# A fused attention and MLP kernel: the softmax epsilon added on ScalarE, and the split of the sinks' values spread over two iterations

## The chip, the cores and the metric

The kernel runs on one core of a Trainium2 chip. The metric is device time in microseconds (us), lower is better. TensorE (PE) multiplies matrices, VectorE (DVE), ScalarE (ACT) and GpSimd (POOL) work elementwise, SyncE (SP) issues DMAs. Each engine takes its instructions strictly in its own order; semaphores hold an instruction until what it needs is there.

## The reference, cut to what matters

A sliding-window attention with sink columns (2 batches, 8 heads, 768 positions, head size 64; 4 sinks, window 128) feeds a gated MLP with a spatial mixing, and that a second mixer. Only the attention's softmax is touched:

```
scores = np.where(keep, scale * q @ k.T, -1e9)
scores = scores - np.max(scores, axis=-1, keepdims=True)
a = np.exp(scores)
a = a / (np.sum(a, axis=-1, keepdims=True) + 1e-09)
out = a @ v                      # then x @ w_in, layer norm, w_spatial, w_out, two more MLPs
```

## The kernel before, in words

The method `banded` does the attention. A block `j` is 128 queries of one batch (12 blocks); a group `g` is half of a block's heads (four heads, 24 groups). A loop over `n` from -3 to 25 is a software pipeline: iteration `n` transposes the probabilities of group `n` on TensorE (`a_transpose`, tile `tr`) and evicts them (`a_out`: `aT` by ScalarE, `aL` by VectorE), normalises group `n+1` (`sums`, `norm`), computes the scores of group `n+3` (`qk` on TensorE into `sc`, `scores` on VectorE into `s` with the negated row minimum `nm`), takes the exponentials of group `n+2` (`expo` on ScalarE, which also accumulates the four row sums into `sums`), and multiplies group `n-1` with the values (`pv`). Every second iteration a finished block is split into a high and a low part (`x_out`: `xTH`, `xTL`), and the sink columns are prepared (`sink_parts`, `sinks`: `eS`, `fl`, `aS`) and multiplied with the sinks' values `vs` (`sinks_mm`, L320).

Two things lie between. `pump` converts one slab of float64 weights per iteration for n = -1 to 6 (three VectorE instructions, L481, L485, L488, into `wi`; then `flush` in the next iteration: ScalarE `wvH` or `wuH`, L499, and GpSimd `wvL` or `wuL`, L500). `fill` gives TensorE tiles of the first MLP (`psv`, `psu`) as soon as the blocks they need are ready, with a fixed budget per iteration; their evictions are `vf` and `uT` on ScalarE, with the layer norm (`st`, `vf`, `vnH`, `vnL`) on VectorE, ScalarE and GpSimd. The order on each engine is the order of the code: the scheduler is set to manual.

The row sums become reciprocals in `sums`, two small VectorE instructions (L195 and L196, 24 of each). `norm` waits for the reciprocals: GpSimd scales heads 2 and 3 of the group (L246), ScalarE heads 0 and 1 (L250). After that ScalarE goes on to the next exponentials (L234, each followed by a read of its accumulator).

`split_vs` is called twice, in iterations 1 and 13, once per batch: ScalarE copies the sinks' values rounded into `vs` (L156), and VectorE subtracts that from the raw values for 32 of the partitions (L158). The raw values stand in one of the four buffers of the tag `tmp`, which `wi` uses too.

Of the kernel before, what the change touches and what calls it, by code (L numbers as in the profile page):

```python
# [8 lines left out]
F32R = mybir.dt.float32r  # L9
I32 = mybir.dt.int32  # L10
U32 = mybir.dt.uint32
AF = mybir.ActivationFunctionType
ALU = mybir.AluOpType
PSUM = bass.MemoryType.PSUM

P = 128
B, H, S, D = 2, 8, 768, 64
NB = S // P
DM = H * D
# [5 lines left out]
SK = 8  # L25
SR = 3 * 4 * SK
# [10 lines left out]
def f32(ap):  # L37
    return ap.bitcast(F32)


class Kernel:
# [106 lines left out]
            nc.sync.dma_start(out=raw[0:SR], in_=self.vs[b])  # L148
            self.vsraw = raw

    def split_vs(self, b):

        nc = self.nc
        raw = self.vsraw
        t = self.vsb[b] = self.ap.tile([P, DM], F32R, name="vs", tag="vs", bufs=1)
        nc.scalar.activation(out=t[0:SR], in_=raw[0:SR], func=AF.Copy)  # L156
        r = slice(4 * SK, 8 * SK)
        nc.vector.tensor_tensor(out=t[r], in0=raw[r], in1=f32(t[r]), op=ALU.subtract)  # L158

    def slots(self, j):  # L160

# [28 lines left out]
    def sums(self, g):  # L190

        V = self.nc.vector
        r = self.ap.tile([P, 4], F32, name="r", tag="r", bufs=3)
        self.rs[g] = r
        V.tensor_scalar(out=r, in0=self.sm[g], scalar1=1e-9, scalar2=None, op0=ALU.add)  # L195
        V.reciprocal(r, r)  # L196

    def scores(self, g):

# [23 lines left out]
    def expo(self, g):  # L223
        nc = self.nc
        j, ph = divmod(g, 2)
        i = j % NB
        u = KW if i else P
        s, nm = self.ss[g]
        if ph == 0:
            self.e[j] = self.ap.tile([P, H, KW], F32, name="e", tag="e", bufs=2)  # L230
        sm = self.ap.tile([P, 4], F32, name="sums", tag="sums", bufs=3)
        self.sm[g] = sm
        for c in range(4):
            nc.scalar.activation(  # L234
                out=self.e[j][:, 4 * ph + c, :u], in_=s[:, c, :u], func=AF.Exp, bias=nm[:, c : c + 1], scale=-1.0,
                accum_out=sm[:, c : c + 1],
            )

    def norm(self, g):

        nc = self.nc
        j, ph = divmod(g, 2)
        r = self.rs[g]
        w = KW if j % NB else P
        e = self.e[j][:, 4 * ph : 4 * ph + 4, 0:w]
        nc.gpsimd.tensor_tensor(  # L246
            out=e[:, 2:4], in0=e[:, 2:4], in1=r[:, 2:4].unsqueeze(2).to_broadcast([P, 2, w]), op=ALU.mult
        )
        for c in range(2):
            nc.scalar.activation(out=e[:, c], in_=e[:, c], func=AF.Copy, scale=r[:, c : c + 1])  # L250
# [88 lines left out]
    def banded(self):  # L339
        self.q, self.vb, self.vsb, self.ps_s, self.ss, self.e, self.sm, self.rs = {}, {}, {}, {}, {}, {}, {}, {}  # L340
        self.aT, self.ps_x, self.aS, self.dv, self.eS = {}, {}, {}, {}, {}
        NJ = B * NB
        self.kr = self.ap.tile([P, NC4, RING, KW], F32, name="kr")
        self.vf = self.ap, "vf", 2
        self.scalar_loads(self.cp)
        self.load_qk(0, 2)
        self.warm(10)
        self.load_qk(1)
        self.prefetch()
        self.load_v(0)  # L350
        self.load_qk(2)
        self.masks(self.ap)
        for n in range(-LQ, NG + 2):
            j, ph = divmod(n, 2)
            self.xdone = self.xnext
            if ph and n >= -1:
                if (n + 7) // 2 < NJ:
                    self.load_qk((n + 7) // 2)
                if (n + 3) // 2 < NJ:
                    self.load_v((n + 3) // 2)  # L360
            if 0 <= n + LN < NG:
                self.sums(n + LN)
            if 0 <= n < NG:
                self.a_transpose(n)
                self.a_out(n)
            if 0 <= n + LN < NG:
                self.norm(n + LN)
            if n + LQ < NG:
                self.qk(n + LQ)
                if n < 0:  # L370
                    self.warm(3)
                self.scores(n + LQ)
            if 0 <= n + LE < NG:
                self.expo(n + LE)
            if 0 <= n < NG and ph == 0 and j % NB:
                self.v_step(j)
                self.sink_parts(j)
            if n in (1, 13):
                self.split_vs(n // 12)
            self.step()  # L380
            if n in PUMPS:
                self.pump()
            if n == max(PUMPS) + 1:
                self.flush()
            if 0 <= n - 1 < NG:
                self.pv(n - 1)
                if ph == 0:
                    if (j - 1) % NB:
                        self.sinks_mm(j - 1)

                    self.fill_until(j - 1)
                    self.x_out(j - 1)
            if 0 <= n < NG and ph == 1 and j % NB:
                self.sinks(j)
            if n == NG - 4:
                self.raws = [self.spatial_load(r) for r in range(2)]
            self.fill(BUDGET)
        self.xdone = self.xnext
        self.vf = self.sp, "tmp", 4
# [529 lines left out]
```

## Time and profile before

| | |
|---|---|
| median of 3 runs | 494.08 us (492.68 to 495.11) |
| the profiled execution's own time | 494.1 us |
| its span, first to last instruction | 492.3 us |
| busy: PE, DVE, ACT, POOL | 469.2, 281.2, 178.8, 146.7 us |
| granted TensorE clock, mean over the span | 0.979 |

The attention occupies about the first 140 us; the rest of the span is the MLPs, where TensorE is busy almost throughout. The shares of the whole span say little about the first stage, so it is read on its own below. A row of a timeline gives start, duration, engine, line, operation, and in square brackets how long the engine was idle before it and whom it waited for.

### The profile page before, as it was taken

How to read it: one execution, taken by the hardware profiler on the slowest of the kernel's cores; microseconds unless marked ns; L12 is line 12 of the kernel's file. 1: busy time of each engine (PE TensorE's matmuls, PEld its weight loads, DVE VectorE, ACT ScalarE, POOL GpSimd, SP SyncE). 2: the span in 40 equal slices, each digit the busy share in tenths (PEclk: the TensorE clock that was granted, in tenths of full speed). 3: DMA queues.
4: the chain of work that ended last, by engine and by line, in shares of the span. 5: the costliest groups of instructions: out<-in, count | busy, mean ns of one | idle time of the engine just before them, and what ended most of it. 6: DMA issues, size and time to landing. Idle time of an engine off the chain costs nothing.

```text
span 492.3 us, 6952 instructions
## 1 busy us (share of the span) xinstructions
PE 469.2 (95%) x2562; PEld 392.3 (80%) x2562; DVE 281.2 (57%) x633; ACT 178.8 (36%) x483; POOL 146.7 (30%) x164
## 2 busy tenths in 40 slices
PE   8678899999999999999999989999999999999994
PEld 7356588788898999998888768888888888888883
DVE  5899865775555399937878698666412211311112
ACT  4656777787754323225642122222101210010000
POOL 1355752354354556642543033222100000000000
PEclk9859899999999999999999999999999999999998
DMA  8744132202005023303534044222010000200002
GB/s 258 246 151 152 66 101 95 87 22 87 1 30 185 1 85 87 102 6 116 173 119 137 35 129 128 91 94 73 21 66 1 0 1 0 86 1 0 1 0 92
DMA packets 19722, 38.48 MB, mean 78 GB/s; under 512 B 1824, under 2 KB 8224, under 8 KB 19680
## 3 DMA queue, kind: packets, MB, share of 16 engines
q1 hardware_dynamic: 19248, 37.69, 23.5%
q8 instruction: 22, 0.36, 0.3%
q10 hardware_dynamic: 432, 0.26, 0.2%
q14 instruction: 20, 0.16, 0.1%
HBM read 34.80 MB, written 3.15 MB: 77 GB/s over the span
## 4 chain that ended last, share of the span: by engine, by line
PE 81%; DVE 11%; ACT 5%; issue 1%; POOL 1%; POOLq 0%; ACTq 0%
PE pso L60 7%; PE pso L58 7%; PE pso L59 7%; PE psc L58 6%; PE psc L60 6%; PE psc L59 6%; PE psg L60 3%; PE psg L59 3%; PE psg L58 3%; PE pv L301 3%; PE ps L60 2%; PE ps L58 2%; PE ps L59 2%; ACT e L234 2%; DVE wi L485 2%; PE psu L58 2%
## 5 line engine op out<-in xcount | busy, mean ns | idle before, releaser
L647 DVE SCALAR_TENSOR_TENSOR hh<-psc,hh 128x512 fp32r<-128x512 f32 x36 | 24.9, 691 | 124.6 <-ACT hh L646 124.6
L646 ACT ACTIVATE hh<-psc 128x512 fp32r<-128x512 f32 x36 | 21.5, 597 | 156.0 <-PE psc L60 156.0
L60 PE MATMUL pso<-c2H,hh 128*128 128x512 f32 x144 | 56.3, 391 | 1.9 <-DVE hh L647 1.9
L58 PE MATMUL pso<-c2H,hh 128*128 128x512 f32 x144 | 56.8, 394 | 0.0
L59 PE MATMUL pso<-c2L,hh 128*128 128x512 f32 x144 | 56.1, 390 | 0.0
L488 DVE SCALAR_TENSOR_TENSOR wi<-rawi,wi 128x512 int32<-128x512 int32 (+2 forms) x46 | 40.3, 876 | 1.6
L234 ACT ACTIVATE e<-s,nm 128x136 f32<-128x136 f32 (+1 forms) x96 | 37.6, 393 | 3.9 <-DVE nm L218 3.9
L485 DVE SCALAR_TENSOR_TENSOR wi<-rawi,wi 128x512 int32<-128x512 int32 (+2 forms) x46 | 36.4, 791 | 1.6
L481 DVE TENSOR_SCALAR wi<-rawi 128x512 int32<-128x512 int32 (+2 forms) x46 | 33.4, 726 | 0.7 <-DMA rawi<-in_moe_w_ch 0.5
L60 PEld LDWEIGHTS pso<-c2H,hh 128*128 128x128 f32 x144 | 27.0, 188 | 8.0 <-DVE hh L647 2.3
L58 PE MATMUL psg<-wsTH,vnH 128*128 128x384 f32 x96 | 32.1, 334 | 0.0
L59 PE MATMUL psg<-wsTL,vnH 128*128 128x384 f32 x96 | 32.1, 334 | 0.0
L60 PE MATMUL psg<-wsTH,vnL 128*128 128x384 f32 x96 | 32.1, 334 | 0.0
L500 POOL TENSOR_TENSOR c2L<-wi,c2H 128x512 fp32r<-128x512 f32 x12 | 16.1, 1339 | 52.4 <-ACT c2H L499 52.4
L59 PEld LDWEIGHTS pso<-c2L,hh 128*128 128x128 f32 x144 | 27.1, 188 | 5.4
L58 PEld LDWEIGHTS pso<-c2H,hh 128*128 128x128 f32 x144 | 27.0, 188 | 5.3
L188 PE MATMUL sc<-kr,q 64*128 64x264 f32 (+2 forms) x192 | 28.8, 419 | 0.4 <-DVE nm L218 0.2
L60 PE MATMUL psc<-u2H,c 128*128 128x512 f32 x72 | 28.0, 389 | 0.0
L58 PE MATMUL psc<-u2H,c1H 128*128 128x512 f32 x72 | 28.0, 389 | 0.0
L59 PE MATMUL psc<-u2L,c1H 128*128 128x512 f32 x72 | 28.0, 389 | 0.0
L60 PE MATMUL psc<-u2H,c1L 128*128 128x512 f32 x72 | 28.0, 389 | 0.0
L58 PE MATMUL psc<-u2H,c 128*128 128x512 f32 x72 | 28.0, 389 | 0.0
(143 smaller groups left out, 1120.1 us busy)
## 6 DMA issues: line engine op xcount, KB each, us to landing
rawi<-in_moe_w_ch SPq DMA_DIRECT2D x24, 512.0 KB, 3.4
rawi<-in_moe_w_in SPq DMA_DIRECT2D x8, 512.0 KB, 4.5
v<-in_v SPq DMA_DIRECT2D x12, 256.0 KB, 3.6
out_x<-o SPq DMA_DIRECT2D x12, 256.0 KB, 2.4
kr<-in_k SPq DMA_DIRECT2D x11, 272.0 KB, 4.1
q<-in_q SPq DMA_DIRECT2D x11, 256.0 KB, 4.2
raws<-in_w_spT SPq DMA_DIRECT2D x6, 384.0 KB, 4.5
rawi<-in_moe_w_out SPq DMA_DIRECT2D x4, 512.0 KB, 5.2
```

The source lines that it names most:

```text
L58: self.nc.tensor.matmul(ps, lh, rh, start=(first and i == 0), stop=False)
L59: self.nc.tensor.matmul(ps, lh, rl, start=False, stop=False)
L60: self.nc.tensor.matmul(ps, ll, rh, start=False, stop=(last and i == n - 1))
L188: nc.tensor.matmul(o, q[r, p, :], k, start=True, stop=True)
L234: nc.scalar.activation(out=self.e[j][:, 4 * ph + c, :u], in_=s[:, c, :u], func=AF.Exp, bias=nm[:, c : c + 1], scale=-1.0, accum_out=sm[:, ...
L301: nc.tensor.matmul(ps[h * D : (h + 1) * D, p, :], w[:, (2 * p + h) * D : (2 * p + h + 1) * D], self.aT[g][c][:, 2 * x + h, :], start=(p == ...
L481: V.tensor_scalar(out=wi, in0=hi, scalar1=3, scalar2=0x3FFFFFFF, op0=ALU.logical_shift_left, op1=ALU.bitwise_and,)
L485: V.scalar_tensor_tensor(out=wi, in0=hi, scalar=-0x40000000, in1=wi, op0=ALU.bitwise_and, op1=ALU.bitwise_or)
L488: V.scalar_tensor_tensor(out=wi, in0=lo, scalar=29, in1=wi, op0=ALU.logical_shift_right, op1=ALU.bitwise_or)
L500: self.nc.gpsimd.tensor_tensor(out=dl, in0=w, in1=f32(dh), op=ALU.subtract)
L646: nc.scalar.activation(out=h, in_=ps, func=AF.Relu)
L647: nc.vector.scalar_tensor_tensor(out=l, in0=ps, scalar=0.0, in1=f32(h), op0=ALU.max, op1=ALU.subtract)
```

## The change

The addition of 1e-9 leaves VectorE: `expo` ends with one ScalarE instruction that adds it to the four row sums in place (24 times), and `sums` is a reciprocal alone. `split_vs` is called in two parts: the copy on ScalarE in iterations 2 and 14, the subtraction on VectorE in iterations 3 and 15.

```
 def split_vs(self, b, part):
     raw = self.vsraw
+    if part == 0:
         t = self.vsb[b] = self.ap.tile([P, DM], F32R, name="vs", tag="vs", bufs=1)
         nc.scalar.activation(out=t[0:SR], in_=raw[0:SR], func=AF.Copy)
+    else:
+        t = self.vsb[b]
         r = slice(4 * SK, 8 * SK)
         nc.vector.tensor_tensor(out=t[r], in0=raw[r], in1=f32(t[r]), op=ALU.subtract)
...
 def sums(self, g):
-    V.tensor_scalar(out=r, in0=self.sm[g], scalar1=1e-9, scalar2=None, op0=ALU.add)
-    V.reciprocal(r, r)
+    V.reciprocal(r, self.sm[g])
...
 def expo(self, g):
     for c in range(4):
         nc.scalar.activation(... func=AF.Exp, ..., accum_out=sm[:, c : c + 1])
+    nc.scalar.activation(out=sm, in_=sm, func=AF.Copy, bias=1e-9)
...
-            if n in (1, 13):
-                self.split_vs(n // 12)
+            if n in (2, 3, 14, 15):
+                self.split_vs(n // 12, n % 2)
```

How the instructions now stand, at three places. In the changed kernel line numbers are two or three higher (L196 is L198, L218 is L220, L250 is L253, L481 is L484). First VectorE in iteration 1, from the last score to the reciprocals of group 2 and on; before:

```order
L218 ISA s,nm<-sc,m_141 128x136
L218 ISA nm 128x1
L158 TENSOR_TENSOR vs<-vsraw,vs 32x512 [waits DMAHW0_49,Activation_49]
L481 TENSOR_SCALAR wi<-rawi 128x512 [waits DMAHW1_49]
L485 SCALAR_TENSOR_TENSOR wi<-rawi,wi 128x512 [waits DVE_49]
L488 SCALAR_TENSOR_TENSOR wi<-rawi,wi 128x512 [waits DVE_49]
L195 TENSOR_SCALAR r<-sums 128x4 [waits Pool_49]
L196 RECIPROCAL r<-r 128x4 [waits DVE_49]
L278 TENSOR_TENSOR aL<-tr,lowT 128x512 [waits Activation_49]
```

The same place on VectorE in the changed kernel:

```order
L220 ISA s,nm<-sc,m_141 128x136
L220 ISA nm 128x1
L484 TENSOR_SCALAR wi<-rawi 128x512 [waits DMAHW1_49]
L488 SCALAR_TENSOR_TENSOR wi<-rawi,wi 128x512 [waits DVE_49]
L491 SCALAR_TENSOR_TENSOR wi<-rawi,wi 128x512 [waits DVE_49]
L198 RECIPROCAL r<-sums 128x4 [waits Activation_49,Pool_49]
L281 TENSOR_TENSOR aL<-tr,lowT 128x512 [waits Activation_49]
```

The subtraction with its wait for ScalarE is gone from here, and one of the two small instructions in front of `aL`. Next ScalarE, from the exponentials of iteration 1 to those of iteration 2 and what follows; before:

```order
L234 ACTIVATE e,sums<-s,nm 128x136 x4
L156 ACTIVATE vs<-vsraw 96x512 [waits DMAHW0_49]
L499 ACTIVATE wvH<-wi 128x512
L275 ACTIVATE aT<-tr 128x512 [waits PE_49]
L250 ACTIVATE e<-e,r 128x136 [waits DVE_49,Activation_49]
L250 ACTIVATE e<-e,r 128x136 [waits Activation_49]
L234 ACTIVATE e,sums<-s,nm 128x136 [waits Pool_49]
L234 ACTIVATE e,sums<-s,nm 128x136 x3
L257 ACTIVATE eS<-e 128x2x32 [waits Activation_49,Pool_49]
L499 ACTIVATE wvH<-wi 128x512
L329 ACTIVATE xTH<-pv 128x4x128 [waits PE_49]
```

The same place on ScalarE in the changed kernel:

```order
L236 ACTIVATE e,sums<-s,nm 128x136 x4
L240 ACTIVATE sums<-sums 128x4 [waits Activation_49]
L502 ACTIVATE wvH<-wi 128x512
L278 ACTIVATE aT<-tr 128x512 [waits PE_49]
L253 ACTIVATE e<-e,r 128x136 [waits DVE_49]
L253 ACTIVATE e<-e,r 128x136
L236 ACTIVATE e,sums<-s,nm 128x136 [waits Pool_49]
L236 ACTIVATE e,sums<-s,nm 128x136 x3
L240 ACTIVATE sums<-sums 128x4 [waits Activation_49]
L260 ACTIVATE eS<-e 128x2x32 [waits Pool_49]
L157 ACTIVATE vs<-vsraw 96x512 [waits DMAHW0_49]
L502 ACTIVATE wvH<-wi 128x512
```

A new instruction (L240) that waits for ScalarE's own accumulators stands behind each group's exponentials, and the copy `vs` now stands in front of the `wvH` and `xTH` of iteration 2. Last VectorE in iteration 3, before:

```order
L218 ISA s,nm<-sc,m_141 128x136
L218 ISA nm 128x1
L481 TENSOR_SCALAR wi<-rawi 128x512 [waits DMAHW6_49]
L485 SCALAR_TENSOR_TENSOR wi<-rawi,wi 128x512 [waits DVE_49]
L488 SCALAR_TENSOR_TENSOR wi<-rawi,wi 128x512 [waits DVE_49]
L195 TENSOR_SCALAR r<-sums 128x4 [waits Activation_49,Pool_49]
L196 RECIPROCAL r<-r 128x4 [waits DVE_49]
```

And the same place on VectorE in the changed kernel:

```order
L220 ISA s,nm<-sc,m_141 128x136
L220 ISA nm 128x1
L161 TENSOR_TENSOR vs<-vsraw,vs 32x512 [waits DMAHW0_49]
L484 TENSOR_SCALAR wi<-rawi 128x512 [waits DMAHW6_49,Pool_49]
L488 SCALAR_TENSOR_TENSOR wi<-rawi,wi 128x512 [waits DVE_49]
L491 SCALAR_TENSOR_TENSOR wi<-rawi,wi 128x512 [waits DVE_49]
L198 RECIPROCAL r<-sums 128x4 [waits Activation_49]
```

The subtraction stands here now, ahead of the weight conversion, and the first conversion waits for GpSimd as well, since its buffer is another one of the four.

## Rows read from the trace of the kernel before

**Rows 1.** Stretches: length, busy PE, PEld, DVE, ACT, POOL; granted clock, DMA share, GB/s

```profile
10.00:21.20 11.20, 7.19 (x54) 4.50 (x52) 10.28 (x41) 7.64 (x30) 3.62 (x4) 1.00 1.02 335
21.20:34.90 13.70, 9.46 (x50) 6.28 (x47) 12.16 (x38) 9.05 (x33) 6.64 (x8) 0.50 0.43 145
34.90:55.30 20.40, 16.58 (x130) 11.83 (x130) 19.62 (x56) 13.38 (x46) 12.78 (x15) 1.00 0.40 131
55.30:58.80 3.50, 3.50 (x22) 2.87 (x23) 3.40 (x11) 1.63 (x8) 3.00 (x5) 0.51 0.01 2
57.00:165.00 108.00, 106.98 (x782) 89.51 (x781) 65.70 (x230) 73.54 (x235) 50.12 (x73) 0.99 0.21 69
```

**Rows 2.** PE's waits from 12 to 160 us: total, times, longest

```profile
PE pv L301 <- DVE xTL L330: 4.4, 4, 1.6
PE tr L267 <- ACT e L250: 4.0, 2, 2.3
PE tr L267 <- DVE aL L278: 3.5, 2, 3.3
PE psu L58 <- ACT aS L313: 0.6, 1, 0.6
```

**Rows 3.** PE in order of time, three of its waits

```profile
55.18 0.57 PE L301 MATMUL pv<-aT,v 128*64 128x128 f32 x4 [1.58 <-DVE xTL L330]
...
69.29 0.44 PE L58 MATMUL psu<-xTH,wuH 128*128 128x384 f32 x1 [0.57 <-ACT aS L313]
...
107.93 0.44 PE L301 MATMUL pv<-aT,v 128*64 128x128 f32 x4 [0.18 <-DVE xTL L330]
```

**Rows 4.** Busy time of line 195 alone, 12 to 57 us

```profile
12.00:57.00 45.00, 3.70 (x8) 0.83 0.52 170
```

**Rows 5.** VectorE in order of time, 14 to 31 us

```profile
14.15 0.16 DVE L195 TENSOR_SCALAR r<-sums 128x4 f32<-128x4 f32 x1
14.35 0.18 DVE L196 RECIPROCAL r<-r 128x4 f32<-128x4 f32 x1
...
18.02 1.23 DVE L195 TENSOR_SCALAR r<-sums 128x4 f32<-128x4 f32 x1
...
22.39 0.68 DVE L158 TENSOR_TENSOR vs<-vsraw,vs 32x512 fp32r<-32x512 f32 x1 [1.13 <-ACT vs L156]
23.10 1.43 DVE L481 TENSOR_SCALAR wi<-rawi 128x512 int32<-128x512 int32 x1
...
30.97 0.64 DVE L195 TENSOR_SCALAR r<-sums 128x4 f32<-128x4 f32 x1
```

**Rows 6.** GpSimd in order of time, 17 to 61 us

```profile
17.48 1.75 POOL L500 TENSOR_TENSOR wvL<-wi,wvH 128x512 fp32r<-128x512 f32 x1 [2.19 <-ACT wvH L499]
...
22.95 1.29 POOL L500 TENSOR_TENSOR wvL<-wi,wvH 128x512 fp32r<-128x512 f32 x1 [2.77 <-ACT wvH L499]
...
53.94 1.72 POOL L551 TENSOR_TENSOR vnL<-vf,vnH 128x512 fp32r<-128x512 f32 x1
...
60.10 1.27 POOL L500 TENSOR_TENSOR wuL<-wi,wuH 128x512 fp32r<-128x512 f32 x1 [1.64 <-ACT wuH L499]
```

**Rows 7.** VectorE in order of time, 55 to 60 us

```profile
55.05 0.68 DVE L542 BATCH_NORM_STATS2 st<-vf 128x6 f32<-128x512 f32 x1
...
60.08 0.18 DVE L196 RECIPROCAL r<-r 128x4 f32<-128x4 f32 x1
```

**Rows 8.** ScalarE in order of time, around 28 and 90 us

```profile
28.45 0.19 ACT L234 ACTIVATION_READ_ACCUMULATOR e<-s,nm 128x1 f32 x1
28.55 0.24 ACT L257 ACTIVATE eS<-e 128x64 fp32r<-128x64 f32 x1
...
90.25 0.62 ACT L156 ACTIVATE vs<-vsraw 96x512 fp32r<-96x512 f32 x1
90.77 0.58 ACT L532 ACTIVATE vf<-psv 128x512 f32<-128x512 f32 x1
```

**Rows 9.** DMA issues of the weights: count, size, median us to landing

```profile
rawi<-in_moe_w_in SPq DMA_DIRECT2D x8, 512.0 KB, 4.5
```

More of the change, by code (lines that the diff above doesn't have):

```diff
@@ L149, in load_v @@
             self.vsraw = raw
-    def split_vs(self, b):
+    def split_vs(self, b, part):
         nc = self.nc
         raw = self.vsraw
[L155 to L158, printed above, removed]
+        if part == 0:
+            t = self.vsb[b] = self.ap.tile([P, DM], F32R, name="vs", tag="vs", bufs=1)
+            nc.scalar.activation(out=t[0:SR], in_=raw[0:SR], func=AF.Copy)
+        else:
+            t = self.vsb[b]
+            r = slice(4 * SK, 8 * SK)
+            nc.vector.tensor_tensor(out=t[r], in0=raw[r], in1=f32(t[r]), op=ALU.subtract)
     def slots(self, j):
@@ L194, in sums @@
         self.rs[g] = r
-        V.tensor_scalar(out=r, in0=self.sm[g], scalar1=1e-9, scalar2=None, op0=ALU.add)
-        V.reciprocal(r, r)
+        V.reciprocal(r, self.sm[g])
     def scores(self, g):
@@ L237, in expo @@
             )
+        nc.scalar.activation(out=sm, in_=sm, func=AF.Copy, bias=1e-9)
     def norm(self, g):
@@ L377, in banded @@
                 self.sink_parts(j)
-            if n in (1, 13):
-                self.split_vs(n // 12)
+            if n in (2, 3, 14, 15):
+                self.split_vs(n // 12, n % 2)
             self.step()
```

## The prediction

> **What bounds the kernel now.** I read the busy times by stretch first, since shares of the whole span mix stages [rows 1]. From 57 to 165 us TensorE is busy 106.98 of 108 us: whatever VectorE saves there is hidden, and the MLPs behind it are TensorE's too. From 21.2 to 55.3 us it is the other way round: VectorE is busy 12.16 of 13.7 and 19.62 of 20.4 us, and TensorE leaves 4.2 and 3.8 us empty. TensorE's waits say for whom [rows 2]: for `xTL` and `aL`, which are VectorE's, and for ScalarE's scaled probabilities, which wait for VectorE's reciprocals. They come to 11.9 us, of which the last one inside the attention's first third ends at 55.18 us [rows 3]. So the change is worth what it takes off VectorE's chain before 55 us, less what it puts on ScalarE where TensorE waits for ScalarE afterwards: 0.57 us at 69.29 for `aS`, and 0.18 us at 107.93 for `xTL` [rows 3].
>
> **The additions that leave VectorE.** From 12 to 57 us there are 8 of them, busy 3.70 us [rows 4]; the last stands behind the wait that ends at 55.18 us and counts for nothing, so 7. An undisturbed one costs VectorE 0.20 us, from its start at 14.15 to the reciprocal's start at 14.35 [rows 5]: 7 x 0.20 = 1.4 us. Two of the seven were held: the one at 18.02 took 1.23 instead of 0.16 us and ended at 19.25, when GpSimd's `wvL` ended (17.48 + 1.75 = 19.23) [rows 5, 6]; the one at 30.97 took 0.64. That is another 1.07 + 0.48 = 1.55 us, but only if the reciprocal that now stands in that place is not held the same way. No row shows a reciprocal that starts under a GpSimd operation with two inputs, so this is bounded: 0 to 1.55 us. Two rows speak for 1.55. The statistics at 55.05, one input from SBUF, ran 0.55 us under `vnL` (until 55.66) and took 0.68 us as ever [rows 6, 7]. And the `wuL` that began at 60.10, 20 ns into the reciprocal of 60.08, took 1.27 us, no more than the free one at 22.95 (1.29), so the reciprocal held nothing against GpSimd either [rows 6, 7]. I take 1.55.
>
> The Trainium skill, "SBUF — State Buffer", section "Who interferes with whom", says that VectorE and GpSimd exclude each other on one shared pair of ports, that copies, casts and tensor_scalar can enter the two-port modes that need it, and that an instruction outside these modes with at most one SBUF input does not contend. The trace agrees for the held additions (1.23 us under `wvL`) and for the statistics (0.68 us under `vnL`). The page does not name the reciprocal among either; by this rule it is free if it has no two-port mode, and held if it has one, which is the second case below.
>
> **The wait that leaves iteration 1.** VectorE sat idle 1.13 us for ScalarE's `vs` ahead of 22.39 [rows 5]: all of that goes, since in iteration 3 the copy is an iteration old. The subtraction itself (0.68 us) is only moved, from one VectorE-bound iteration to another: 0. The conversion behind it took 1.43 us from 23.10, held by the `wvL` of 22.95 to 24.24 [rows 5, 6]: 1.1 us at most. Without wait and subtraction VectorE gets to the conversions some 1.8 us sooner, and the `wvL`, which had to wait for `wvH` behind `vs` on ScalarE, comes only some 0.3 us sooner; it then falls under the third conversion as in iteration 0, and GpSimd waits instead. 0 to 1.1, I take 1.0.
>
> **What ScalarE gets.** The new instruction has four elements; the nearest rows are the accumulator read of one (0.19 us) and `eS` of 64 (0.24 us) [rows 8]. It must wait for the last accumulator: `eS` started 0.10 us after that read began, while the new one can start only when it has ended, 0.19 us plus a hand-over of about 0.035 us (the gap between addition and reciprocal, 14.31 to 14.35). What follows it on ScalarE is then 0.19 + 0.035 + 0.10 - 0.10 = about 0.23 us later; the upper bound, with nothing overlapped, is 0.19 + 0.035 + 0.24 = 0.47. The reciprocal could wait for it: 0 to 0.23 us each. I take 0 in the first stage, since no addition there shows a wait [rows 5] and ScalarE is busy 9.05 of 13.7 us [rows 1]. Queued behind it are `wvH`/`wuH`, `xTH`, `aS`, `vf`. In iteration 2 the copy `vs` (0.52 us from 90.25 to the next start [rows 8]) is ahead of `xTH` too: 0.75 us in all, of which `xTL` loses between 0 and 0.75, as far as `xTH` had no lead; ScalarE's idle third of that stretch makes me take 0.2. In iteration 3 GpSimd's half of a weight comes 0.23 later and the conversions, one subtraction later, fall under it: 0 to 1.1 (the hold of 23.10); I take 0.2, as if they had been held before too.
>
> First stage: 1.4 + 1.55 + 1.13 + 1.0 - 0.4 = 4.7 us off VectorE's chain.
>
> **What TensorE can take of it.** From 21.2 to 34.9 us its granted clock is 0.50, the 1.2 GHz level, after a stretch in which it was busy 7.19 of 11.2 us [rows 1]. That earlier stretch hardly changes, so I expect the same low level. If VectorE runs 4 us ahead by 31 us, up to 4 us of TensorE's work that was done at the full level moves into the low one and takes twice as long for half of the room: 0 to 2 us lost, I take 1.1. So 3.6 us by 55 us. The next to be late would be the weights, 4.5 us from issue to landing [rows 9]; with two buffers they are asked for nearly two iterations ahead, and an undisturbed one takes 3.67 us (14.35 to 18.02 [rows 5]), so two take 7.3: I take 0.
>
> **Given back after 57 us.** TensorE's wait at 69.29 is for `aS`, directly behind exponentials: + 0.23; the like place one block later, for which the list has no wait, 0 to 0.23: + 0.23. Toward 107.93 a chain of ScalarE and VectorE runs through iterations 13 to 17; it loses the second wait for `vs`, gets the copy (0.52) in iteration 14, the subtraction in 15 and 0.23 three times, and saves 0.20 per reciprocal: + 0.5. Bounds for all this: 0 (if TensorE has work in hand) to 3.7, below. Sum 1.0.
>
> Total: -3.6 + 1.0 = -2.6. The profiled execution took 494.1 us, 1.8 more than its span and within 0.1 of the median 494.08: 494.1 - 2.6 = 491.5 us.
>
> **Rivals.**
> Second case, the reciprocal is held like the addition. Then 1.55 falls away, and in iteration 1 a new hold of about 1.3 us appears behind a `wvL` that now runs past the conversions: 4.7 - 1.55 - 1.3 = 1.85, less 0.5 for the low clock, less 1.0 later: -0.4, 493.7 us. For it: nothing measured under GpSimd; against it: `wuL` at 60.10.
>
> Third, ScalarE becomes the bound after 57 us. If each of the 14 iterations from 8 to 21 passes its 0.23 us on to TensorE, and the chain to 107.93 its 0.5: 3.2 + 0.5 = 3.7, so +0.1, 494.2 us. For it: the wait for `aS`, where there is no lead. Against it: ScalarE is busy 73.54 of 108 us there [rows 1]. The Trainium skill speaks against the change here: "ScalarE: Activation LUTs", section "Rules for kernel authors", puts adds on VectorE, not ScalarE; the section "What ACT_TABLE_LOAD costs" gives 186 ns plus 0.833 ns per element with immediate operands, an estimate of 0.19 us here, which no run so far shows.
>
> Fourth, more than forecast: the second low stretch, 55.3 to 58.8 us at 0.51 with TensorE busy throughout [rows 1], goes away because TensorE idles less before it. That gives 1.7 us more: 489.8 us.
>
> Fifth, slower: the shifted pattern costs TensorE another stretch at 1.2 GHz like that of 13.7 us, where it has work throughout; half of it is 6.85 us: 491.5 + 6.85 = 498.3. It decides if TensorE, at some place ahead of it, idles as it does from 10 to 21 us (busy 0.64); nothing in the change adds such idle time, which speaks against it.
>
> **How the numbers follow.** Forecast 0.45 (its own range 490.3 to 493.0), second 0.12, third 0.15, fourth 0.20, fifth 0.08. About 0.5%, 2.5 us, is what a measurement can tell from no change, so the border lies at 491.6, next to the forecast, which I split 0.25 faster and 0.20 same. Faster: 0.25 + 0.20 = 0.45; same: 0.20 + 0.12 + 0.15 = 0.47; slower 0.08. The range runs from 489.4, under the fourth case's middle, to 495.0, over the third's; the fifth and the tail of the fourth are left out.
>
> **What would show it.** Reciprocals of 0.18 us under `wvL`; no wait of VectorE for `vs`; TensorE's waits before 57 us down from about 12 to about 8 us; the new instruction near 0.19 us with what follows 0.23 us later; waits for `aS` of about 0.8 and 0.3 us. I am wrong if a reciprocal takes over 0.5 us, if VectorE waits for ScalarE's sums before 55 us, or if the granted clock after 57 us has a new low stretch.

## The result: 488.8 us, twice the forecast gain

The changed kernel takes 488.77 us (median of 4 runs, 487.84 to 489.52) against 494.08 us: a ratio of 0.989, 95% interval 0.9865 to 0.9914, or 4.2 to 6.7 us less. The forecast was 2.6 us less. The profiled execution took 489.52 us, the longest of the four, at a span of 487.7 us, 4.6 us less than that of before; its trace shows where they are.

The stretches of [rows 1] in the changed kernel, and below them three stretches at one granted clock each (columns as there):

```profile
10.00:21.20 11.20, 8.21 (x58) 4.70 (x56) 10.61 (x42) 9.43 (x37) 3.43 (x5) 0.96 1.03 342
21.20:34.90 13.70, 12.73 (x80) 9.01 (x80) 12.95 (x41) 10.35 (x39) 9.92 (x10) 0.66 0.50 166
34.90:55.30 20.40, 17.59 (x124) 12.76 (x125) 17.93 (x59) 14.87 (x53) 14.61 (x18) 0.92 0.36 113
...
57.00:165.00 108.00, 106.16 (x774) 89.85 (x771) 60.84 (x200) 72.08 (x234) 47.58 (x68) 1.00 0.22 69
...
20.40:30.60 10.20, 9.23 (x48) 5.89 (x45) 9.86 (x33) 8.67 (x31) 7.74 (x8) 0.50 0.63 211
30.70:51.10 20.40, 17.59 (x146) 12.84 (x145) 19.43 (x57) 14.58 (x51) 13.63 (x16) 1.00 0.41 131
51.20:54.50 3.30, 3.30 (x9) 2.50 (x8) 2.14 (x12) 2.54 (x11) 2.59 (x5) 0.50 0.01 2
```

From 10 to 35 us TensorE did 138 matmuls instead of 104: the same work came sooner. The first stretch at 1.2 GHz is there again, but ends at about 30.6 instead of 34.9 us. The second is there too, 4 us sooner; so the fourth rival did not come about, though its figure, 489.8 us, lies nearer to the measured time than the forecast's. VectorE is still the full engine from 30.7 to 51.1 us, 19.43 of 20.4. Behind 57 us TensorE is empty for 1.84 us where before it was for 1.02.

TensorE's waits from 12 to 160 us (total, times, longest), to be held against [rows 2], and four of them in order of time, against [rows 3]:

```profile
PE pv L304 <- DVE xTL L333: 3.7, 4, 1.7
PE tr L270 <- ACT e L253: 2.4, 2, 1.5
PE psu L58 <- ACT aS L316: 1.1, 2, 0.8
...
```

```profile
49.62 0.44 PE L304 MATMUL pv<-aT,v 128*64 128x128 f32 x4 [1.75 <-DVE xTL L333]
...
63.97 0.44 PE L58 MATMUL psu<-xTH,wuH 128*128 128x384 f32 x1 [0.81 <-ACT aS L316]
...
74.38 0.44 PE L58 MATMUL psu<-xTH,wuH 128*128 128x384 f32 x1 [0.32 <-ACT aS L316]
...
103.20 0.44 PE L304 MATMUL pv<-aT,v 128*64 128x128 f32 x4 [0.54 <-DVE xTL L333]
```

The `pv` that began at 55.18 us begins at 49.62: 5.56 us sooner. 0.35 us of that lie ahead of iteration 0's first transpose (11.28 after 11.63 us) and are put down to the execution, not to the change: the other kernels start it at 11.14 to 11.50 us, those that keep every addition on VectorE (split_only, before_late) at 11.19 and 11.17. 5.2 us are the change's. The wait in front of this `pv` is still for `xTL`, and no shorter (1.75 after 1.58): TensorE does not limit here. Its waits before 57 us fell from 11.7 to 6.2 us, where about 8 were forecast. Then some is given back: `aS` at 63.97 is waited for 0.24 us longer than at 69.29 before, the one at 74.38 is new, and the wait at 103.20 is 0.36 us longer. From there to the end the lead is 4.7 us.

VectorE from 13 to 26 us, its reciprocals and the first conversion of iteration 2, and GpSimd's weights and `dv` beside them, against [rows 5, 6]:

```profile
13.79 0.17 DVE L198 RECIPROCAL r<-sums 128x4 f32<-128x4 f32 x1
...
17.46 0.17 DVE L198 RECIPROCAL r<-sums 128x4 f32<-128x4 f32 x1
...
21.13 0.17 DVE L198 RECIPROCAL r<-sums 128x4 f32<-128x4 f32 x1
...
23.63 0.85 DVE L484 TENSOR_SCALAR wi<-rawi 128x512 int32<-128x512 int32 x1
...
26.45 0.16 DVE L198 RECIPROCAL r<-sums 128x4 f32<-128x4 f32 x1
```

```profile
17.09 1.59 POOL L503 TENSOR_TENSOR wvL<-wi,wvH 128x512 fp32r<-128x512 f32 x1 [2.44 <-ACT wvH L502]
...
20.78 1.58 POOL L503 TENSOR_TENSOR wvL<-wi,wvH 128x512 fp32r<-128x512 f32 x1 [1.50 <-ACT wvH L502]
...
22.92 1.27 POOL L288 TENSOR_TENSOR dv<-v 128x512 f32<-128x512 f32 x1
```

The reciprocals at 17.46 and 21.13 start inside a `wvL` (17.09 to 18.68, 20.78 to 22.36) and take 0.17 us. From reciprocal to reciprocal, iterations 0 and 1 take 3.67 us each, where they took 4.94 and 6.80 in the kernel before (from 14.35 to 19.29, and from there to 26.09):

```profile
19.29 0.18 DVE L196 RECIPROCAL r<-r 128x4 f32<-128x4 f32 x1
...
26.09 0.18 DVE L196 RECIPROCAL r<-r 128x4 f32<-128x4 f32 x1
```

Iteration 2 has a new hold: its first conversion starts under the `dv` of 22.92 and takes 0.85 instead of 0.42 us.

### The profile page after: what moved, and what is told of

It reads as the page before. It is cut to its first block, busy times and chain, and to the rows that moved or that the text cites. A ratio compares the mean times of both kernels' runs of the same rounds, so it can differ in the third digit from the quotient of the medians.

```text
span 487.7 us, 6920 instructions
## 1 busy us (share of the span) xinstructions
PE 469.0 (96%) x2562; PEld 391.9 (80%) x2562; DVE 274.5 (56%) x609; ACT 183.2 (38%) x507; POOL 147.0 (30%) x164
## 4 chain that ended last, share of the span: by engine, by line
PE 82%; DVE 9%; ACT 5%; issue 1%; POOL 1%; POOLq 0%; ACTq 0%
PE pso L60 7%; PE pso L58 7%; PE pso L59 7%; PE psc L60 6%; PE psc L59 6%; PE psc L58 6%; PE psg L60 3%; PE psg L59 3%; PE psg L58 3%; PE pv L304 3%; PE ps L60 2%; PE ps L58 2%; PE ps L59 2%; PE psu L58 2%; PE sc L191 2%; ACT e L236 2%
## 5 line engine op out<-in xcount | busy, mean ns | idle before, releaser
L484 DVE TENSOR_SCALAR wi<-rawi 128x512 int32<-128x512 int32 (+2 forms) x46 | 32.8, 714 | 0.7 <-DMA rawi<-in_moe_w_ch 0.7
```

Of the source, the lines that this page charges most:

```text
L484: V.tensor_scalar(out=wi, in0=hi, scalar1=3, scalar2=0x3FFFFFFF, op0=ALU.logical_shift_left, op1=ALU.bitwise_and,)
```

## The experiments

"Lead" is how much sooner than in the profiled execution of before TensorE starts the same work: first at the `pv` of 55.18 us, then at the end; for the changed kernel 5.56 and 4.69 us. One profiled execution gives it; medians stand with their ratio to the kernel before run beside them, 95% interval behind it.

**The addition alone (eps_only), the split alone (split_only).**

```
-            if n in (2, 3, 14, 15):
-                self.split_vs(n // 12, n % 2)
+            if n in (1, 13):
+                self.split_vs(n // 12, 0)
+                self.split_vs(n // 12, 1)
```

> The addition on ScalarE alone; the sinks' values are split in iterations 1 and 13 as before. Theory A (VectorE's chain sets the first 55 us; holds by GpSimd count as much as the instructions): seven additions x 0.20 = 1.4 us, two holds at 18.02 and 30.97 worth 1.55, a third hold (0.96 us, third conversion of iteration 4) gone because ScalarE's eS comes 0.2 us later, less 0.7 given back after 57 us: 3.2 us, 491 us; the wait for vs (1.13 us) stays. Theory B (the moved subtraction does nearly all): 493 us or more, and TensorE's pv of iteration 6 no more than 1.5 us earlier than in the kernel before.

490.88 us, 0.9946 (0.9926 to 0.9966), lead 3.00 and 2.29 us. The second iteration still waits for `vs` and has its conversion held:

```profile
20.70 0.68 DVE L161 TENSOR_TENSOR vs<-vsraw,vs 32x512 fp32r<-32x512 f32 x1 [1.31 <-ACT vs L157]
21.41 1.41 DVE L485 TENSOR_SCALAR wi<-rawi 128x512 int32<-128x512 int32 x1
```

The other half: the kernel before, with `split_vs` in two parts.

```
-        V.reciprocal(r, self.sm[g])
+        V.tensor_scalar(out=r, in0=self.sm[g], scalar1=1e-9, scalar2=None, op0=ALU.add)
+        V.reciprocal(r, r)
...
-        nc.scalar.activation(out=sm, in_=sm, func=AF.Copy, bias=1e-9)
```

> The split in two iterations alone; the addition stays on VectorE. Theory A: the wait of 1.13 us and about 1.0 us of hold behind it go, the additions are held as before: TensorE's pv of iteration 6 some 2 us earlier, 492 us, and the third conversion of iteration 4 is still held (about 1.65 us) since ScalarE is no later there. Theory B: 4 us or more of the 5.3, 490 us or less.

491.56 us, 0.9967 (0.9951 to 0.9982), lead 2.76 and 2.59 us. Here the additions are held as before, now by 1.2 us in two iterations instead of one:

```profile
17.58 1.26 DVE L198 TENSOR_SCALAR r<-sums 128x4 f32<-128x4 f32 x1
...
22.55 1.23 DVE L198 TENSOR_SCALAR r<-sums 128x4 f32<-128x4 f32 x1
```

The leads of the parts come to 5.76 us, the whole's is 5.56, but that they add up is partly chance: some 0.4 us of each lead is the start's. By iteration (reciprocal to reciprocal) the addition alone takes 1.27 us off iteration 0 and 0.03 off iteration 1, the split alone nothing and 1.86; together they take off 1.27 and 3.13, since only together is the hold at 22.55 spared. In iteration 4, on the other hand, either part alone does away with the hold: its third conversion takes 1.65 us in the kernel before and 0.69 in both. Here the expectation missed, as split_only was to keep it; that hold does not hang on the addition's place alone (the table at the end of this section shows on what).

What eps_only gained so in iteration 4 it mostly lost again in the same place: the iteration took 6.96 us after 7.20. In this kernel two stretches at 1.2 GHz lay before 35 us, the second from 26.3 to 33.1 us, and VectorE waited for `aT`, which follows TensorE's transposes, 1.17 us; in the changed kernel it waited 0.38 (eps_only, then the changed kernel):

```profile
35.63 0.69 DVE L281 TENSOR_TENSOR aL<-tr,lowT 128x512 f32<-128x512 f32 x1 [1.17 <-ACT aT L278]
```

```profile
33.07 0.69 DVE L281 TENSOR_TENSOR aL<-tr,lowT 128x512 f32<-128x512 f32 x1 [0.38 <-ACT aT L278]
```

**The 1e-9 nowhere (no_eps), and twice (eps_twice).** The first leaves the addition out altogether; the second adds 5e-10 two times over on ScalarE.

> As the changed kernel, but 1e-9 is added nowhere (that part of the computation is left out), so ScalarE is spared the 24 instructions. Theory A: after 57 us the 0.85 us that the changed kernel gives back shrink to about 0, but in iteration 4 GpSimd gets ahead of the third conversion again and holds it for 0.96 us: no difference, 488.8 us, with the hold seen in the profile. Rival C (the instruction only costs): 0.85 us faster than the changed kernel, 487.9 us, no such hold.

> As the changed kernel, with 5e-10 added twice on ScalarE, so the suspected cost doubles. Theory A: TensorE's waits for aS at iterations 9 and 11 grow by another 0.23 us each and the one for xTL at iteration 17 by up to 0.3: 0.8 us slower than the changed kernel, 489.6 us. Rival D (ScalarE has room): no difference, 488.8 us.

Without it: 487.33 us, 0.9876 (0.9845 to 0.9908), by the intervals not told apart from the changed kernel; lead 4.60 us at the `pv` and 4.85 at 141 us: behind 57 us nothing is given back. Its one profiled execution had another 3.4 us at 1.2 GHz from 287 us on, so its end says nothing. At the `pv` it is 1 us behind the changed kernel although it does less, and iteration 4 takes 7.24 instead of 6.17 us: on GpSimd the cast of `eS` starts ahead of VectorE's first conversion, `wuL` follows at 36.35, and the third conversion takes 1.64 us again:

```profile
35.69 0.24 POOL L260 CAST eS<-eS 128x64 fp32r<-128x64 f32 x1 [0.86 <-ACT eS L259]
```

```profile
35.76 0.45 DVE L483 TENSOR_SCALAR wi<-rawi 128x512 int32<-128x512 int32 x1
...
36.97 1.64 DVE L490 SCALAR_TENSOR_TENSOR wi<-rawi,wi 128x512 int32<-128x512 int32 x1
```

The hold is what theory A expected; the median lies with rival C. Twice: 492.0 us, 0.9958 (0.9941 to 0.9976), lead 5.04 and 2.73 us, 2.4 us slower than expected. What is given back, 2.3 us, is in three waits of TensorE:

```profile
64.80 0.44 PE L58 MATMUL psu<-xTH,wuH 128*128 128x384 f32 x1 [1.11 <-ACT aS L317]
...
75.46 0.44 PE L58 MATMUL psu<-xTH,wuH 128*128 128x384 f32 x1 [0.55 <-ACT aS L317]
...
105.13 0.44 PE L305 MATMUL pv<-aT,v 128*64 128x128 f32 x4 [1.39 <-DVE xTL L334]
```

One addition raises each wait for `aS` by 0.24 to 0.32 us, the second by 0.23 to 0.30. The chain toward `xTL` takes 0.36 us for the first and 0.85 for the second.

**The addition on ScalarE only for groups 0 to 7 (eps_mixed).**

```
+        if g < 8:
+            nc.scalar.activation(out=sm, in_=sm, func=AF.Copy, bias=1e-9)
...
```

In `sums`, groups 8 and up get their VectorE addition back.

> The changed kernel, but 1e-9 is added on ScalarE for groups 0 to 7 alone, and on VectorE for groups 8 to 23, whose sums come after TensorE has become the bound. Theory A: the first stage as in the changed kernel, and most of the 0.85 us given back after 57 us is kept: 0.6 us faster than the changed kernel, 488.2 us. Rival G (VectorE's chain to iteration 17 takes back what ScalarE is spared): no difference, 488.8 us.

487.94 us, 0.9891 (0.9869 to 0.9914): 0.7 us under the changed kernel run beside it (after_again), with intervals that overlap: not told apart. Executions at the same granted clock took the same time (0.983: 489.52 here, 489.67 there; 0.986: 488.59, and 488.56 and 489.11). In the trace TensorE's wait for `xTL` falls from 0.54 to 0.30 us, the second one for `aS` is gone from its list, and the first rises from 0.81 to 1.28 us; from 60 to 141 us 0.46 us of the lead is given back, in after_again 0.86. Ahead of the first `aS`, ScalarE's scaling at 59.65 waits 0.60 us for VectorE's reciprocal, a wait that after_early, with these additions on ScalarE, does not have: this is rival G's path, and that it makes the whole rise is not shown.

**The changed kernel again, and with TensorE kept busy (after_again, warm_after).** The second gets four extra matmuls in each of iterations 0 to 2, whose results nothing reads.

```
+                elif n < 3:
+                    self.warm(4)
```

> The changed kernel once more, as the measure for the other three on the same chip: 0.989 of the kernel before, 488.8 us.

> The changed kernel with four extra 128x128 matmuls, whose result nobody reads, in each of iterations 0, 1 and 2, where TensorE sits idle for 1 to 2 us. They take what the change did to TensorE's idle time further. Theory A (TensorE's idle time sets the length of the stretch at 1.2 GHz, and this length sets what the first stage gains): the low stretch from 20 us gets shorter than 10.2 us or goes, and with it up to 1 us at TensorE's pv of iteration 6; 488 us. Rival E (the low stretch has its length whatever TensorE does there): it stays at 10.2 us, the extra matmuls cost 0 to 2 us; 489 to 491 us.

Again: 488.67 us, 0.9898 (0.9877 to 0.992). In its profiled execution the second stretch at 1.2 GHz lay not at 51 but at 287 us; the lead was 5.45 us at the `pv`, 7.0 at 60 us, and 4.50 at the end. The stretch moves some 1.5 us from one place to another and changes nothing in the sum. With the matmuls: 489.51 us, 0.9915 (0.9893 to 0.9938), no better. Yet the first stretch at 1.2 GHz is gone altogether (stretches as above, then TensorE's waits from 12 to 160 us):

```profile
10.00:21.20 11.20, 10.22 (x74) 6.96 (x73) 10.75 (x43) 9.35 (x38) 3.52 (x5) 1.00 1.04 342
21.20:34.90 13.70, 11.57 (x96) 8.27 (x94) 13.29 (x44) 10.81 (x41) 9.75 (x10) 1.00 0.52 162
```

```profile
PE pv L304 <- DVE xTL L333: 5.9, 4, 2.0
```

The lead is 6.21 us at the `pv`, 0.65 more, and 4.94 at the end. 0.14 of the 0.65 is the start's; 0.50 is iteration 4's, which takes 5.67 instead of 6.17 us, since `aL` no longer waits for `aT`. TensorE's waits for `xTL` grew instead, from 3.7 to 5.9 us. Of the lead's 0.65, 0.40 is lost at 287 us, where TensorE waits 2.30 instead of 1.90 us for `hh`, behind a conversion for which the weights came late (VectorE waited 0.60 us for their DMA at 283.54). So theory A holds for the stretch and the `pv`, and not for the time.

**The second half of a weight's conversion ahead of the exponentials (flush_first).** This should keep GpSimd's half away from the third conversion.

```
+            if n in PUMPS:
+                self.flush()
```

> The changed kernel with the second half of the weight conversion (ScalarE wvH or wuH, GpSimd wvL or wuL) put ahead of the exponentials, for n from -1 to 6, so that GpSimd is through before VectorE converts the next slab. Theory A (holds by GpSimd are on the chain): the two holds of 1.0 us left in iterations 3 and 5 go, TensorE's pv of iteration 6 comes 1 to 2 us earlier than in the changed kernel, 487.5 us. Rival F (the holds are hidden, or dv takes their place): no difference, 488.8 us.

493.12 us, 0.9986 (0.9967 to 1.0006), lead 2.52 and 1.63 us: it loses nearly all of the gain. The holds do not go, they fall on the first and second conversions, in more iterations:

```profile
15.55 1.19 DVE L486 TENSOR_SCALAR wi<-rawi 128x512 int32<-128x512 int32 x1
...
25.66 1.64 DVE L490 SCALAR_TENSOR_TENSOR wi<-rawi,wi 128x512 int32<-128x512 int32 x1
```

**Iteration 4 by itself (before_late, after_early).** Iteration 4 gets 1.03 us shorter by the change; the forecast had 0.2 us for it. Each trace gives the start on GpSimd of the cast of `eS` and of the weight's half `wuL`, and on VectorE that of the first and of the third conversion. In the kernel before, GpSimd and then VectorE:

```profile
39.85 0.24 POOL L258 CAST eS<-eS 128x64 fp32r<-128x64 f32 x1 [0.63 <-ACT eS L257]
40.04 0.52 POOL L259 TENSOR_TENSOR eS<-e,eS 128x64 fp32r<-128x64 f32 x1
40.52 1.72 POOL L500 TENSOR_TENSOR wuL<-wi,wuH 128x512 fp32r<-128x512 f32 x1
```

```profile
37.46 0.69 DVE L278 TENSOR_TENSOR aL<-tr,lowT 128x512 f32<-128x512 f32 x1 [0.19 <-ACT aT L275]
...
39.87 0.49 DVE L481 TENSOR_SCALAR wi<-rawi 128x512 int32<-128x512 int32 x1
...
41.14 1.65 DVE L488 SCALAR_TENSOR_TENSOR wi<-rawi,wi 128x512 int32<-128x512 int32 x1
```

In the changed kernel:

```profile
35.64 0.35 POOL L261 CAST eS<-eS 128x64 fp32r<-128x64 f32 x1 [1.00 <-ACT eS L260]
35.95 0.85 POOL L262 TENSOR_TENSOR eS<-e,eS 128x64 fp32r<-128x64 f32 x1
36.76 1.74 POOL L503 TENSOR_TENSOR wuL<-wi,wuH 128x512 fp32r<-128x512 f32 x1
```

```profile
35.47 0.42 DVE L484 TENSOR_SCALAR wi<-rawi 128x512 int32<-128x512 int32 x1
...
36.66 0.69 DVE L491 SCALAR_TENSOR_TENSOR wi<-rawi,wi 128x512 int32<-128x512 int32 x1
```

Before, the cast starts 0.02 us ahead of the first conversion; `eS` is through quickly (0.24 and 0.52 us), `wuL` starts 0.62 us ahead of the third conversion, and that one waits: 1.65 us. After, the cast starts 0.17 us behind it, the subtraction of `eS` takes 0.85 us, `wuL` starts 0.10 us behind the third conversion, and it is GpSimd that waits. To test it, the kernel before got one more ScalarE instruction in all, which changes no value:

```
+        if g == 6:
+            nc.scalar.activation(out=sm, in_=sm, func=AF.Copy, bias=0.0)
```

> The kernel before, with one more ScalarE instruction in all: a copy of the four softmax sums onto themselves behind the exponentials of group 6 (whose probabilities for the sinks are cast on GpSimd in iteration 4); VectorE keeps all its additions. Theory A (one microsecond of the change's gain is the race of iteration 4: whether GpSimd has the cast of eS before VectorE starts the first conversion): eS comes about 0.2 us later, the cast starts behind the first conversion's start, GpSimd's half of the weight comes later, and the third conversion takes 0.69 us instead of the 1.65 us it took in the kernel before. TensorE's pv of iteration 6 (55.18 us in the kernel before) then starts about 0.9 us sooner, though nothing was taken off any engine; at the end of the program 0.5 to 0.9 us are left. Rival B (the hold of iteration 4 went because VectorE was quicker over the first iterations, by the additions and the wait for vs): the hold stays (over 1.4 us), and the pv of iteration 6 starts 0 to 0.3 us later than before.

493.02 us, 0.9981 (0.9964 to 0.9999): the medians lie 1.0 us apart, the interval ends just under 1, and the fastest execution took 492.18 us with the instruction and without it. Lead 1.80 us at the `pv` and 1.77 at the end. Its GpSimd and VectorE in iteration 4:

```profile
39.62 0.72 POOL L260 CAST eS<-eS 128x64 fp32r<-128x64 f32 x1 [0.86 <-ACT eS L259]
```

```profile
39.10 0.42 DVE L483 TENSOR_SCALAR wi<-rawi 128x512 int32<-128x512 int32 x1
...
40.28 0.69 DVE L490 SCALAR_TENSOR_TENSOR wi<-rawi,wi 128x512 int32<-128x512 int32 x1
```

The cast is 0.52 us behind, the third conversion takes 0.69 us, and the `pv` starts 1.80 us sooner, 0.46 of it the start's. Of the other 1.34 us, more than the 0.9 expected, 0.96 are the third conversion's (1.65 less 0.69), and 0.28 come from `aL`, which starts 0.09 us behind the reciprocal instead of 0.37. The first four iterations are as long as before, so theory B falls: the order of the starts decides the hold. But this run does not show that the instruction turned the order. Its stretches at 1.2 GHz lay elsewhere (the last before 50 us ended at 29.6 instead of 34.9 us), so that `aL` did not wait for `aT`: counted from the reciprocal, the cast came 0.23 us later than in the kernel before, and the first conversion 0.31 us sooner. Either was enough. The counterpart, the changed kernel with group 6's addition back on VectorE:

> The changed kernel, with the addition of 1e-9 for group 6 alone back on VectorE. Theory A: the cast of eS in iteration 4 comes 0.2 us sooner, ahead of VectorE's first conversion; GpSimd's half of the weight starts sooner and the third conversion of iteration 4 takes about 1.65 us again instead of 0.69 us. TensorE's pv of iteration 6 starts 0.9 to 1.2 us later than in the changed kernel (4.4 to 4.7 us ahead of the kernel before instead of 5.5), and the median is 0.5 to 1 us above the changed kernel's 488.7. Rival B (it is the pace of the first iterations): the third conversion of iteration 4 stays at 0.69 us, and only the addition's 0.2 us is lost.

489.26 us, 0.9912 (0.9879 to 0.9944), not told apart from the changed kernel. Theory A's figure missed: the third conversion stayed at 0.69 us. Its premise failed too: the cast came sooner (35.13), but so did the first conversion (34.91), since the subtraction `aL` no longer waited 0.38 us for `aT`, and the cast stayed 0.22 us behind. So this run doesn't separate the theories. All eleven profiled executions with that order of code on VectorE together do, and they also keep apart the two things that move the starts (iteration 4; the added ScalarE instructions are those behind group 6's exponentials; the last two columns are the start of the cast, counted from that of the first conversion, and the time of the third conversion, in us):

| run | added on ScalarE | `aL` waited for `aT` | cast behind first conversion | third conversion |
|---|---|---|---|---|
| no_eps | 0 | 0.48 | -0.07 | 1.64 |
| before | 0 | 0.19 | -0.02 | 1.65 |
| after | 1 | 0.38 | 0.17 | 0.69 |
| after_again | 1 | 0.41 | 0.16 | 0.69 |
| eps_only | 1 | 1.17 | 0.16 | 0.69 |
| eps_twice | 2 | 0.54 | 0.40 | 0.69 |
| after_early | 0 | 0 | 0.22 | 0.69 |
| split_only | 0 | 0 | 0.29 | 0.69 |
| eps_mixed | 1 | 0 | 0.46 | 0.69 |
| warm_after | 1 | 0 | 0.47 | 0.69 |
| before_late | 1 | 0 | 0.52 | 0.69 |

Where the cast came first the conversion was held, in both cases; where it came 0.16 to 0.52 us behind, it was not, in all nine. Among like rows each added instruction moves the cast back by some 0.24 us; a wait for `aT` moves it forward by some 0.3, since it holds up VectorE more than ScalarE and GpSimd (counted from the reciprocal, the first conversion comes 0.59 us later in no_eps than in after_early, the cast 0.30). The wait follows the place of the stretch at 1.2 GHz: where it ended 2.2, 1.9, 1.8, 1.7, 1.6 and 1.2 us ahead of the reciprocal that opens iteration 4 (before, after, after_again, no_eps, eps_twice, eps_only), `aL` waited 0.19, 0.38, 0.41, 0.48, 0.54 and 1.17 us; where it ended 3.7 us or more ahead, or was missing, it did not wait. The changed kernel and no_eps, with that stretch in nearly the same place (20.4 to 30.6 and 20.8 to 31.0 us), differ by the instruction alone: there it is what spares the hold.

## Why the prediction was wrong

**Right: the mechanism, and the larger terms.** Iteration 0 got 1.27 us shorter, the forecast 0.20 + 1.07: the reciprocal is not held, and the second rival falls. The Trainium skill, "SBUF — State Buffer", section "Who interferes with whom", left the reciprocal open; the 0.17 us under `wvL` put it among the instructions that do not contend, while the third conversion, with two inputs from SBUF, was held (1.65 us). Iteration 1 got 3.13 us shorter; 0.20 + 1.13 + 1.0, and the moved subtraction's 0.7, make 3.0. One reading was off, without a consequence: the statistics at 55.05 ran 0.61 us under `vnL`, not 0.55.

**Right: the price on ScalarE.** The new instruction and its neighbours, to be held against [rows 8]:

```profile
35.00 0.19 ACT L236 ACTIVATION_READ_ACCUMULATOR e<-s,nm 128x1 f32 x1
35.23 0.21 ACT L240 ACTIVATE sums<-sums 128x4 f32<-128x4 f32 x1
35.34 0.24 ACT L260 ACTIVATE eS<-e 128x64 fp32r<-128x64 f32 x1
```

The new instruction waits for the accumulator's end (35.19) and 0.04 us more, takes 0.21 us, and `eS` starts 0.34 us behind the accumulator's start instead of 0.10: 0.24 us, forecast 0.23. Given back were 0.24 + 0.32 at the two `aS` by the waits (0.23 each by TensorE's starts) and 0.36 at `xTL`: 0.8 to 0.9, forecast 1.0. ScalarE did not become the bound, so the third rival falls. The Trainium skill's preference for adds on VectorE ("ScalarE: Activation LUTs", section "Rules for kernel authors") does not hold in the first 55 us (eps_only took 1.27 us off iteration 0 there), and does hold behind 57 us, where the addition costs 0.8 us and takes nothing off TensorE's path. The estimate of 0.19 us that the prediction worked out from the Trainium skill ("ScalarE: Activation LUTs", section "What ACT_TABLE_LOAD costs") stands beside 0.20 to 0.21 measured.

**Wrong, the step that failed: "What TensorE can take of it", 1.1 us.** I took the stretch at 1.2 GHz as fixed in length and TensorE as full in it. Neither was so: it came out 3.5 us shorter in this execution (10.2 after 13.7), and behind it TensorE still waits for VectorE (for `xTL`, 0.60 us at 38.01 and 1.75 at 49.62). What was measured: VectorE waited 0.38 us for `aT` at 33.07, where before it had waited 0.19, so 0.2 us; and with the stretch removed (warm_after) the `pv` came 0.5 us sooner, the start's 0.14 taken off, and the time got no shorter. The term was there in kind, and in eps_only, with the stretch at another place, it had the forecast's size (1.17 us of waiting). But it works through VectorE's waits for `aT`, not through a lack of room on TensorE, and where the stretch falls varies from kernel to kernel.

**Wrong, a term that was missing: the hold of iteration 4.** I had read it in no row, since I looked only for holds of the additions and of the conversion at 23.10. The forecast's sum had 0.2 us for this iteration; it gave 1.03. The change did not aim at it: it shifted two starts against each other by 0.2 us, from -0.02 to 0.17. That this fell on the right side is luck; the added instruction alone is worth 0.24 us there, and in the kernel before the hold goes too when the low stretch lies elsewhere (before_late: 0.52, of which its instruction is some 0.24).

**Smaller.** Iteration 2 gained 0.23 instead of 0.48 us by the new hold at 23.63; iteration 3 lost 0.61 instead of 0.7. Together: 3.6 + 1.1 + 0.8 (iteration 4, the 0.2 us for `aT` taken off already), less 0.3 for the small ones, makes 5.2 us, the measured 5.56 less the start's 0.35; less 0.87 given back, 4.3, and with the start's 0.35 the 4.7 of the profiled executions. The medians differ by 5.3 us; what lies between is within the interval.

The fifth rival did not come about either: from 57 to 165 us the granted clock is 1.00, where [rows 1] has 0.99.

## What to carry to other kernels

Take a lost clock off a gain only as far as the others wait for the engine that runs at it: read that from their waits behind the slow stretch. Where two engines hold each other, list every held instruction of the bound engine, in each iteration, with the distance to the start that decided it: a hold decided by 0.02 us is worth a term of its own, as a chance, for any change that shifts either engine. An instruction on a filled engine is worth moving to one with room, but only for the iterations in which that engine is the bound; here the traces say so (no_eps gives nothing back behind 57 us, eps_twice 2.3 us), while the time of eps_mixed, the kernel that does it, is not told apart.

## What the hardware showed that I had not expected

One ScalarE instruction of 0.2 us made iteration 4 1.07 us shorter (the changed kernel against no_eps, 6.17 and 7.24 us), by letting VectorE's third conversion start ahead of GpSimd's `wuL`. In these rows the third conversion, where it starts first, keeps its 0.69 us, and the one that starts second pays: 1.65 instead of 0.69 us on VectorE, 1.74 instead of 1.29 on GpSimd. (In the kernel before `wuL` pays as well, 1.72 us, since it starts under the second conversion, 40.40 to 41.11.) On VectorE that delays TensorE here. On GpSimd it does not: from iteration 4's end, the reciprocal, to the `pv` it is 10.94 us in the changed kernel with the `wuL` of 1.74 us, and 10.96 in warm_after with one of 1.29.

A stretch of 3.4 us at 1.2 GHz stands at about 51 us in one execution of the changed kernel and at 287 us in another, with TensorE busy throughout both times:

```profile
51.20:54.50 3.30, 3.30 (x21) 2.50 (x20) 2.35 (x13) 3.27 (x14) 2.58 (x5) 1.00 0.01 2
286.80:290.20 3.40, 3.40 (x9) 2.64 (x9) 3.33 (x5) 0.63 (x1) 1.39 (x2) 0.50 0.41 131
```

These are of the second execution (after_again): 21 matmuls in the 3.3 us in which the first had 9. Whoever compares two traces at one moment only, between these two places, is 1.5 us off. Why it moves, no run here shows.
